# Attention's opening in another order, and the landmark sums of its second head group by other means

## The chip, the cores and the metric

The kernel runs on one core of a Trainium2 chip. The metric is the device time of one execution in microseconds, as the median of several runs. The engines are TensorE (PE in the profile, its weight loads PEld), VectorE (DVE), ScalarE (ACT), GpSimd (POOL) and SyncE (SP), which issues the DMAs.

## The reference

Three layers follow each other. The first is a Nyström attention over 4 batches, 8 heads, 576 tokens and 64 dimensions a head, with 32 landmarks that are means over 18 tokens; the other two are feed-forward layers over all 2304 tokens.

```
q_lm, k_lm = means of q and k over 18 tokens each
A  = softmax(scale * q    k_lm^T)
Bm = softmax(scale * q_lm k_lm^T)
C  = softmax(scale * q_lm k^T)
Z  = Bm^T / (norm1(Bm) * norminf(Bm) + 1e-6);  6 times: Z = 2Z - Z Bm Z
x  = A Z C v                       # 2304 tokens x 512
x  = mish(x w_in) w_out            # 512 -> 2048 -> 512
h  = x w2_in;  s = h * softmax(h);  out = (layernorm(s) * g_ln) w2_out
```

## The kernel before

The heads of a batch are worked on in two groups of four (g = 0 and 1). Batch 0 is done first, in small steps, so that the first feed-forward layer can begin; the other batches' attention is spread over that layer later. `A` of the attention is kept apart from the rest: the product of `Z C v` with the first weights is folded into a matrix `u` (`u_step`, L751), and the hidden layer is computed as `A^T` times `u` (`gemm1`, L760). All large products are split in a high and a low part, three products for one.

The weights arrive as 64-bit floats and are decoded on the chip, block by block (sixteen blocks of 1 MB for the first layer, in the order `order1`). A block goes through a scale step on ACT (`s`, L151), an exponent step on ACT (`e`, L159), one or two merges on DVE (`m`, `f`, L171 and L178) and, for the second weight matrix, a split on ACT and DVE (`m` ends with L252, `l` is L130).

The order of PE, ACT and DVE in the opening is written out by hand: `PSEQ` is a list of step names, and the instructions of each engine stand in the order in which the steps name them. No engine overtakes within its own queue. A trailing digit 0 or 1 after a name of the attention is the head group; for `s`, `e`, `f`, `m` and `l` it is the weight block, and for `G`, `M`, `S` and `Y` it is the pair of hidden tiles:

- `lq`, `lk`: landmark sums of q and k (`prep`). Group 0 sums on DVE (L386); group 1 has PE add up 18 products of the identity with every 18th column, 64 columns each (L383), and ACT copy the sum out (L384).
- `cs`, `as`, `bs`: the scores of C, A and Bm (L419, L512, L410). `cm`, `bm`: their maxima on DVE and exponentials on ACT (L461 to L468, L430 to L435). `bn`, `bu`, `bz`, `bb`, `ni`: norms of Bm, with column sums on PE (L447, L448), and the start of the iteration. `p1` to `p6` and `q1` to `q6`: its six steps, small products on PE (L328) and an addition on DVE (L130).
- `ct`, `cn`, `cv`: the transposed C, its row sums, and C v. `w`: the product with Z.
- `ta`, `tb` with a digit: transposition of the two halves of A's scores (L517). `sm`, `sn`, `sl`: softmax of the first half; `sx`, `sy`, `sz`: of the second. (`tb` without a digit loads ACT's table for Mish.)
- `u`, `u1`: folding of the weights. `G`, `M`, `S`, `Y`: hidden product, Mish (L789), split (L797 on ACT, L130 on DVE) and second product (L812) of a pair. `ld` is where SP issues the DMAs of six later weight blocks (into tiles that hold batch 0's q, k and v before).

Behind `PSEQ` the steps of the remaining pairs, decode steps and the other batches' attention are planned by counters. Those of them that the framework may move ahead are kept behind the step named `EDGE` (`Y1`). PSUM is taken in turn: four banks `y0` to `y3` for the attention's scores, a pair of banks `a`, and a tile `h` of two banks, of which there is one, so a hidden product waits until Mish has read the one before it.

Of the kernel before, what the change touches and what calls it, by code (L numbers as in the profile page):

```python
# [14 lines left out]
AF = mybir.ActivationFunctionType  # L15
ALU = mybir.AluOpType
AX = mybir.AxisListType
# [10 lines left out]
def nystrom_moe_kernel(  # L28
# [13 lines left out]
    V, A, PE, G, SP = nc.vector, nc.scalar, nc.tensor, nc.gpsimd, nc.sync  # L42
# [5 lines left out]
    L = 32  # L48
    R = S // L
# [27 lines left out]
    ident, swap = wheel[:, 0:P], wheel[:, D:]  # L77
# [154 lines left out]
    def w1_items():  # L232
        def item(side, m):
            if side == "i":
                s, a = divmod(m, 2)
                n = 2 * NQ
                return words((w_in, w_raw)[a](s)), w_in(s)[:, a * n:(a + 1) * n], lambda c: None, lambda c: None
            return parts(wr["o", m], wop, f"wo{m}", lambda x: wo.update({m: x}))

        return [lambda x=x: item(*x) for x in order1]  # L240
# [89 lines left out]
    def attn(b, g):  # L330
# [3 lines left out]
        T, lm, x = {}, {}, {}  # L334
# [9 lines left out]
        def ps(k=None):  # L344
            if first and k is None:
                bank_n[0] += 1
                return ps_y.tile([P, 512], F32, tag=f"y{bank_n[0] % 4}", name="pa")
            if first and k == "e" and g == 1:
                bank_n[1] += 1
                return ps_h.tile([P, 2, 512], F32, tag="h", name="pa")[:, bank_n[1] % 2]  # L350
            return ps_a.tile([P, 512], F32, tag="a", name="pa")
# [14 lines left out]
        def view_of(nm):  # L366
            T[nm] = raw[nm, b, g].rearrange("p (h s) -> p h s", h=2)

        def prep(nm):
            if nm not in T:  # L370
                view_of(nm)
            n = "qk".index(nm)
            if not lms or not first and not n:
                lms[:] = [att.tile([P, 2 * P + L], F32, tag="lm", name="lm")]
            t = x["lm"] = lms[0]
            if first:
                o = (2 * g + n) * 2 * L
                lm[nm] = t[:, o:o + 2 * L].rearrange("p (j h l) -> p j h l", j=1, h=2)
                src = T[nm].rearrange("p h (l r) -> p h l r", r=R)
                if g:  # L380
                    pt = ps("e")[:, 0:2 * L].rearrange("p (h l) -> p h l", h=2)
                    for r in range(R):
                        PE.matmul(pt, lhsT=ident, rhs=src[:, :, :, r], start=r == 0, stop=r == R - 1)  # L383
                    A.activation(out=lm[nm][:, 0], in_=pt, func=AF.Copy)  # L384
                else:
                    V.tensor_reduce(out=lm[nm][:, 0], in_=src, op=ALU.add, axis=AX.X)  # L386
            else:
                lm[nm] = t[:, n * P:(n + 1) * P].rearrange("p (j h l) -> p j h l", j=2, h=2)
                V.tensor_reduce(out=own(n), in_=T[nm].rearrange("p h (j l r) -> p h j l r", j=2, r=R), op=ALU.add, axis=AX.X)
            yield  # L390

        def own(n):

            d = x["lm"][:, n * P:(n + 1) * P + L].rearrange("p (j i) -> p j i", j=2)[:, :, 0:2 * L]
            return d.rearrange("p j (h l) -> p h j l", h=2)[:, :, :, 0:L // 2]
# [207 lines left out]
        def whole():  # L603

            yield from prep("q")
            for _ in prep("k"):
                cross()
                yield
# [31 lines left out]
        def opening():  # L640
# [55 lines left out]
            def soften(r0):  # L696
                sg[r0] = soft(r0, RH)
                next(sg[r0])
                next(sg[r0])

            r = {"lq": lambda: spin(prep("q")), "lk": lambda: spin(prep("k")), "bs": bs, "bm": bm, "bn": b_norm, "bb": bb, "bu": bu,
                 "bz": lambda: b_scale(px[1][:, 0:2 * L]), "ni": lambda: n_first(px[0]), "as": a_scores,
                 "ta": lambda: a_turn(0), "tb": lambda: a_turn(1), "sm": lambda: soften(0), "sn": lambda: next(sg[0]), "sl": lambda: spin(sg[0]),
# [21 lines left out]
    OWN = ()  # L725
    ONE = tuple(range(8))
    US = 1
    W2R = 0.6
    LAG = 3
    GB = 3  # L730
# [26 lines left out]
    def mm3(o, pairs):  # L757
# [4 lines left out]
    hb, gb, yb = {}, {}, {}  # L762
    ps_x = []
    PSEQ = """
        lq0 cs0 lk0 bs0 bm0 cm0 as0 lq1 tb0 bn0 ta0 s0 bb0 bu0 cs1 bz0 ct0 lk1 bs1 cn0 sm0 ni0 p10 cm1 bm1 q10 sn0 s1 p20 bn1 as1 bb1 e0 cn1 q20 e1
        s2 bu1 bz1 p30 q30 ni1 ct1 e2 tb1 p11 ta1 p40 q11 s3 p21 sx0 q40 e3 q21 sm1 p31 p50 cv0 q50 q31 m0 s4 p60 p41 q41 q60 p51 q51 cv1 e4 w0
        sn1 p61 q61 m1 w1 ld sl1 s5 sl0 u e5 G0 s6 m3 s7 sx1 tb M0 e6 m4 m2 m5 sy1 u1 l2 G1 M1 G2 S0 e7 S1 M2 l5 e8 m6 sz1
        Y0 sy0 G3 M3 sz0 s8 S2 l6 Y1 G4 S3 e9 M4 m7 Y2 G5 s9 l7 S4 M5 f8 Y3 m8 S5 f9 G6 Y4 M6 G7 Y5 m9 M7 S6"""
    GLB = 2
    HX = 1  # L770
    U = NCH * NF
# [60 lines left out]
    with ExitStack():  # L832
# [19 lines left out]
        w1, part = decode(w1_items(), lambda: att.tile([P, R * D], F32, tag="dc", name="dc", bufs=2)[:, 0:2 * DM], OWN, ONE, READY)  # L852
# [3 lines left out]
        def w1_tick():  # L856
            nonlocal done, ticks
            if done < NU:
                ticks += 1
                with behind():  # L860
                    done = next(w1, 10 ** 6)
# [132 lines left out]
        def may_step(u):  # L994
            b, s = steps[0]
            return all((b, g) in aw for g in range(NG)) and (b == 0 or last_use[b - 1, s] < u) and \
                (b > 0 or done > max(pos["i", i] for i in range(4 * s, 4 * s + 4)))

        for p in range(PAIRS, U // 2):
            u = 2 * p + 1  # L1000
            s_, i = units[u]
            c, i0, i1 = segs[s_]

            def tick():
                nonlocal w2n
                nonlocal k4
                if done < NU:
                    k4 += 1
                    want = NT * (p - PAIRS + k4 / 5) / DT
                    while ticks < want and done < NU:  # L1010
                        w1_tick()
                elif w2 and w2n < W2R * (u - w2u):
                    w2n += 1
# [6 lines left out]
            for x in '1sa.u..t2..u':  # L1020
# [10 lines left out]
                elif x == 'u':  # L1031
                    for _ in range(US):
                        if steps and may_step(u + 1):
# [212 lines left out]
```

## Time and profile before

| | us |
|---|---|
| median of 3 runs | 630.76 |
| lowest and highest | 628.88, 631.19 |
| the profiled execution | 628.73 |
| its span, first to last instruction | 627.0 |
| PE busy in the span | 601.1 |
| DVE busy | 374.2 |
| ACT busy | 330.2 |

The profiled execution is one run, and its span leaves out 1.7 us around the program. Busy times of PE are modelled from pipelined instructions, so a busy PE is not PE at its peak. Each written product of 32-bit floats stands as two records in the profile.

### The profile page before, as it was taken

What the parts mean: (1) busy time and instruction counts of PE and PEld (TensorE: products, weight loads), DVE (VectorE), ACT (ScalarE), POOL (GpSimd) and SP (SyncE); (2) the same over time, 40 slices, a digit from 0 to 9 for tenths busy, and PEclk for the clock granted to TensorE, in tenths of its full rate; (3) what the DMA queues carried; (4) which work ended last, traced back from release to release, by engine and by line L of the source; (5) the groups of instructions that cost most, each with busy time, mean ns of one, the idle gap of its engine ahead of it and who ended that gap; (6) DMA issues with size and microseconds to landing.
All of it is one profiled execution on the core that took longest, in us unless ns stands there. A gap on an engine that the chain in (4) does not pass through costs nothing.

```text
span 627.0 us, 11427 instructions
## 1 busy us (share of the span) xinstructions
PE 601.1 (96%) x4560; PEld 521.6 (83%) x4560; DVE 374.2 (60%) x868; ACT 330.2 (53%) x597; POOL 25.7 (4%) x21
## 2 busy tenths in 40 slices
PE   6888899999999999999999999999999999999997
PEld 4648878767999898999889999998888888888886
DVE  4787999755764224764456412555886667657560
ACT  2688975764563434553545533535665544536341
POOL 0000000000000000000132001230000000000000
PEclk9859999999999999999999999999999999999999
DMA  9997220521131100101253102411656444454442
GB/s 343 395 393 279 81 61 17 189 78 50 66 115 39 39 2 1 39 1 36 92 158 109 60 1 87 154 68 55 183 176 194 121 145 141 136 166 117 136 122 97
DMA packets 50453, 74.28 MB, mean 118 GB/s; under 512 B 5088, under 2 KB 38880, under 8 KB 50400
## 3 DMA queue, kind: packets, MB, share of 16 engines
q1 hardware_dynamic: 50400, 73.55, 35.9%
q8 instruction: 36, 0.59, 0.4%
q14 instruction: 17, 0.14, 0.1%
HBM read 54.07 MB, written 19.46 MB: 117 GB/s over the span
## 4 chain that ended last, share of the span: by engine, by line
PE 76%; ACT 9%; DVE 7%; DMA 4%; issue 2%; POOL 1%; POOLq 1%; SPq 0%; ACTq 0%; DVEq 0%
PE h L760 27%; PE y L812 24%; PE po L760 16%; PE pa L751 2%; DMA r<-in_moe_w_out_dram 2%; PE pa L383 1%; POOL r L149 1%; PE pa L500 1%; PE pa L419 1%; DMA r<-in_moe_w_in_dram 1%; ACT hl L252 1%; ACT ro L159 1%; PE pa L584 1%; ACT gh L797 1%; PE pa L328 1%
## 5 line engine op out<-in xcount | busy, mean ns | idle before, releaser
L812 PE MATMUL y<-gh,hl 128*128 128x288 f32 x1024 | 162.2, 298 | 2.6 <-DVE hl L130 1.4
L812 PEld LDWEIGHTS y<-gh,hl 128*128 128x128 f32 x1024 | 142.5, 188 | 13.5 <-issue 8.4
L760 PE MATMUL h<-AT,u 128*128 128x288 f32 x768 | 122.5, 303 | 6.7 <-ACT s L789 4.0
L760 PEld LDWEIGHTS h<-AT,u 128*128 128x128 f32 x768 | 107.3, 190 | 18.0 <-ACT s L789 6.9
L760 PE MATMUL h<-hl,yb 128*128 128x512 f32 x432 | 103.3, 395 | 0.1
L130 DVE SCALAR_TENSOR_TENSOR gl<-s,gh 128x288 fp32r<-128x288 f32 x128 | 53.3, 453 | 81.4 <-ACT gh L797 38.2
L760 PEld LDWEIGHTS h<-hl,yb 128*128 128x128 f32 x432 | 81.2, 188 | 19.3 <-ACT ye L829 0.5
L812 PE MATMUL y<-gl,hl 128*128 128x288 f32 x512 | 90.4, 297 | 0.0
L760 PE MATMUL po<-hl,lh 128*128 128x512 f32 x288 | 88.8, 389 | 0.0
L797 ACT ACTIVATE gh<-s 128x288 fp32r<-128x288 f32 x128 | 50.1, 440 | 48.5 <-PE y L812 48.2
L812 PEld LDWEIGHTS y<-gl,hl 128*128 128x128 f32 x512 | 74.8, 188 | 0.1
L789 ACT ACTIVATE s<-h 128x576 f32<-128x576 f32 x64 | 41.6, 650 | 59.6 <-PE h L760 49.9
L760 PEld LDWEIGHTS po<-hl,lh 128*128 128x128 f32 x288 | 54.1, 188 | 11.5
L1088 ACT ACTIVATE e<-h,st 128x1024 f32<-128x1024 f32 x18 | 20.1, 1117 | 71.9 <-DVE st L1087 71.9
L760 PE MATMUL po<-hl,ll 128*128 128x512 f32 x144 | 56.2, 390 | 0.0
L1086 DVE TENSOR_REDUCE st<-h 128x1 f32<-128x1024 f32 x18 | 22.0, 1223 | 33.7 <-PE h L760 33.7
L1139 DVE TENSOR_TENSOR ll<-lT,lh 128x1024 fp32r<-128x1024 f32 x18 | 22.1, 1225 | 19.1 <-ACT lh L1138 19.1
L130 DVE SCALAR_TENSOR_TENSOR u<-pa,u 128x512 fp32r<-128x512 f32 x32 | 20.7, 686 | 20.2 <-ACT u L754 20.2
L760 PEld LDWEIGHTS po<-hl,ll 128*128 128x128 f32 x144 | 27.0, 188 | 5.6
L178 DVE SCALAR_TENSOR_TENSOR r<-r 128x1024 uint32<-128x1024 uint32 x10 | 12.2, 1225 | 31.5 <-POOL r L149 31.5
L149 POOL TENSOR_SCALAR r<-r 128x1024 f32<-128x1024 f32 x8 | 23.3, 2909 | 139.9 <-DMA r<-in_moe_w_out_dram 58.1
L1096 ACT ACTIVATE s<-s,st 128x1024 f32<-128x1024 f32 x18 | 20.8, 1153 | 9.3 <-DVE st L1094 9.3
(180 smaller groups left out, 653.4 us busy)
## 6 DMA issues: line engine op xcount, KB each, us to landing
lnd<-sT SPq DMA_DIRECT2D x72, 128.0 KB, 2.3
lT<-lnd SPq DMA_DIRECT2D x18, 512.0 KB, 4.1
r<-in_moe_w_in_dram SPq DMA_DIRECT2D x8, 1024.0 KB, 8.2
ro<-in_moe_w_out_dram SPq DMA_DIRECT2D x8, 1024.0 KB, 16.0
yd<-ye SPq DMA_DIRECT2D x32, 144.0 KB, 1.8
y<-yd SPq DMA_DIRECT2D x18, 256.0 KB, 4.4
out_dram<-ob SPq DMA_DIRECT2D x18, 256.0 KB, 3.9
w<-in_moe_w_in_dram SPq DMA_DIRECT2D x4, 1024.0 KB, 10.8
```

Source lines behind the costliest of these rows:

```text
L130: return V.scalar_tensor_tensor(out=out, in0=in0, scalar=1.0, in1=in1, op0=ALU.mult, op1=op)
L149: G.tensor_scalar(out=x, in0=x, scalar1=2.0 ** -112, scalar2=None, op0=ALU.mult)
L178: V.scalar_tensor_tensor(out=t[:, :, 0], in0=t[:, :, 1], scalar=3, in1=t[:, :, 0], op0=ALU.logical_shift_left, op1=ALU.bitwise_or)
L751: PE.matmul(po[g][h * L:(h + 1) * L], lhsT=wb[b][r, g, h * L:(h + 1) * L], rhs=w[r, h], start=True, stop=True)
L760: PE.matmul(o, lhsT=a, rhs=b_, start=i == 0, stop=i == n - 1)
L789: A.activation(out=s, in_=h, func=AF.Mish)
L797: A.activation(out=gh[:, e], in_=s[:, e], func=AF.Copy)
L812: PE.matmul(yb[s_][d][:, 0:N], lhsT=w_out(s, i + e)[:, d * P:(d + 1) * P], rhs=r[:, e], start=i == i0 and e == k == 0, stop=i + 2 == i1 an ...
L1086: V.tensor_reduce(out=st[:, 0:1], in_=h, op=ALU.max, axis=AX.X)
L1088: A.activation(out=e, in_=h, func=AF.Exp, bias=st[:, 1:2], accum_out=st[:, 2:3])
L1096: A.activation(out=s, in_=s, func=AF.Identity, scale=-1.0, bias=st[:, 4:5])
L1139: V.tensor_tensor(out=llv, in0=src, in1=f(lhv), op=ALU.subtract)
```

## The change

Two things change. The sums of group 1: those of q are done by DVE, as for group 0. Those of k are done on PE by three products of the identity with 6 neighbouring columns of each landmark at a time (2 x 32 x 6 = 384 columns), which add up in PSUM and leave 6 partial sums for each landmark; DVE adds these, out of PSUM. And `PSEQ` has the same 141 names in another order.

```
-                if g:
-                    pt = ps("e")[:, 0:2 * L].rearrange("p (h l) -> p h l", h=2)
-                    for r in range(R):
-                        PE.matmul(pt, lhsT=ident, rhs=src[:, :, :, r], start=r == 0, stop=r == R - 1)
-                    A.activation(out=lm[nm][:, 0], in_=pt, func=AF.Copy)
+                if g and n:
+                    pt = ps("e")[:, 0:2 * L * GS].rearrange("p (h l s) -> p h l s", h=2, s=GS)
+                    n = R // GS
+                    for c in range(n):
+                        PE.matmul(pt, lhsT=ident, rhs=src[:, :, :, c * GS:(c + 1) * GS], start=c == 0, stop=c == n - 1)
+                    V.tensor_reduce(out=lm[nm][:, 0], in_=pt, op=ALU.add, axis=AX.X)
                 else:
                     V.tensor_reduce(out=lm[nm][:, 0], in_=src, op=ALU.add, axis=AX.X)
...
+    GS = 6
...
     PSEQ = """
-        lq0 cs0 lk0 bs0 bm0 cm0 as0 lq1 tb0 bn0 ta0 s0 bb0 bu0 cs1 bz0 ct0 lk1 bs1 cn0 sm0 ni0 p10 cm1 bm1 q10 sn0 s1 p20 bn1 as1 bb1 e0 cn1 q20 e1
-        s2 bu1 bz1 p30 q30 ni1 ct1 e2 tb1 p11 ta1 p40 q11 s3 p21 sx0 q40 e3 q21 sm1 p31 p50 cv0 q50 q31 m0 s4 p60 p41 q41 q60 p51 q51 cv1 e4 w0
-        sn1 p61 q61 m1 w1 ld sl1 s5 sl0 u e5 G0 s6 m3 s7 sx1 tb M0 e6 m4 m2 m5 sy1 u1 l2 G1 M1 G2 S0 e7 S1 M2 l5 e8 m6 sz1
-        Y0 sy0 G3 M3 sz0 s8 S2 l6 Y1 G4 S3 e9 M4 m7 Y2 G5 s9 l7 S4 M5 f8 Y3 m8 S5 f9 G6 Y4 M6 G7 Y5 m9 M7 S6"""
+        lq0 cs0 lk0 bs0 as0 lq1 bm0 cm0 bn0 ta0 cn0 s0 e0 bu0 cs1 bz0 sm0 e1 cm1 tb0 lk1 bb0 bs1 m0 ni0 bm1 ct1 p10 as1 sx0 bn1 q10 ta1 s1 bb1 bu1
+        ct0 s2 bz1 p20 q20 p30 ni1 p11 cn1 e2 q30 cv0 q11 sn0 p40 e3 q40 p21 s3 q21 e4 p31 sm1 p50 q31 s4 q50 p41 tb1 q41 p60 p51 q60 s5 q51 p61
+        m1 sn1 w0 cv1 q61 sl1 w1 ld e5 sx1 sl0 u s6 m3 s7 G0 tb m4 M0 m2 m5 sy0 l5 u1 sy1 l2 e6 G1 M1 S0 s8 S1 e7 G2 M2 e8
+        m6 sz0 Y0 sz1 f8 G3 e9 Y1 l6 M3 s9 S2 S3 G4 M4 Y2 m7 G5 S4 l7 M5 m8 Y3 G6 f9 S5 M6 Y4 G7 S6 M7 Y5 m9"""
```

## Rows read from the trace of the kernel before

**Rows 1.** The page, part 1: busy us (share of the span) xinstructions of each engine.

```profile
PE 601.1 (96%) x4560; PEld 521.6 (83%) x4560; DVE 374.2 (60%) x868; ACT 330.2 (53%) x597; POOL 25.7 (4%) x21
```

**Rows 2.** Table by stages: busy us (xinstructions) of each engine, granted clock, DMA.

```profile
core 0: us, PE busy (x) PEld busy (x) DVE busy (x) ACT busy (x) POOL busy (x), PEclk, DMA share, GB/s
11.00:22.10 11.10, 10.94 (x110) 9.82 (x109) 4.09 (x18) 2.12 (x6) 0.00 (x0) 1.00 1.03 377
22.10:50.30 28.20, 20.89 (x285) 12.42 (x285) 23.08 (x66) 26.10 (x44) 0.00 (x0) 0.70 1.03 400
50.30:60.00 9.70, 9.65 (x73) 9.65 (x74) 7.98 (x16) 6.76 (x12) 0.00 (x0) 1.00 0.79 313
60.00:105.00 45.00, 41.90 (x365) 36.97 (x364) 41.52 (x72) 34.63 (x59) 0.00 (x0) 1.00 0.18 55
105.00:300.00 195.00, 191.97 (x1894) 169.93 (x1891) 108.86 (x311) 100.02 (x216) 1.38 (x4) 1.00 0.16 53
```

**Rows 3.** Timeline of PE: start us, us, instruction, [idle before and its releaser].

```profile
50.35 1.87 PE L760 MATMUL h<-AT,u 128*128 128x288 f32 x12 [2.58 <-ACT s L789]
```

**Rows 4.** Timeline of ACT from 15 to 50 us, same columns.

```profile
15.04 0.22 ACT L384 ACTIVATE lm<-pa 128x64 f32<-128x64 f32 x1 [4.43 <-PE pa L383]
...
17.55 0.60 ACT L481 ACTIVATE scr_u<-pa 128x512 f32<-128x512 f32 x1 [1.27 <-PE pa L477]
18.05 0.26 ACT L482 ACTIVATE CT<-pa 64x128 f32<-64x128 f32 x1
21.98 0.22 ACT L384 ACTIVATE lm<-pa 128x64 f32<-128x64 f32 x1 [3.67 <-PE pa L383]
...
23.38 0.29 ACT L435 ACTIVATE scr_u<-pa,st 128x32 f32<-128x32 f32 x1
...
24.67 1.14 ACT L159 ACTIVATE w<-w 128x1024 uint32<-128x1024 uint8 x1
...
26.71 1.12 ACT L151 ACTIVATE ro<-ro 128x1024 f32<-128x1024 f32 x1
...
49.65 0.65 ACT L789 ACTIVATE s<-h 128x576 f32<-128x576 f32 x1
```

**Rows 5.** Chain of waits in order of time: start us, us, what.

```profile
5.84 2.14 PE pa L419 x16
...
8.09 1.92 PE pa L512 x16
10.01 5.00 PE pa L383 x36
...
15.27 0.34 PE pa L447 x2
...
15.83 1.10 PE pa L419 x16
...
17.63 4.33 PE pa L383 x36
```

**Rows 6.** DMA issues at 2.6 and at 16.3 us: KB, us to landing.

```profile
w<-in_moe_w_in_dram SPq DMA_DIRECT2D x1, 1024.0 KB, 8.9
...
ro<-in_moe_w_out_dram SPq DMA_DIRECT2D x1, 1024.0 KB, 17.9
```

**Rows 7.** Timeline of DVE from 4 to 19 us, columns as for PE.

```profile
4.24 2.84 DVE L386 TENSOR_REDUCE lm<-scr_w 128x64 f32<-128x1152 f32 x2 [2.15 <-DMA scr_w<-in_q_dram]
...
11.32 0.24 DVE L444 TENSOR_SCALAR rs<-diag,st 128x32 f32<-128x32 f32 x1
...
18.26 0.81 DVE L461 TENSOR_REDUCE st<-pa 128x1 f32<-128x288 f32 x2
```

**Rows 8.** Table by stages around the low clock, columns as before.

```profile
22.00:28.00 6.00, 4.25 (x89) 2.58 (x89) 4.96 (x25) 6.00 (x13) 0.00 (x0) 1.00 1.02 408
29.00:45.00 16.00, 13.51 (x170) 8.02 (x176) 13.43 (x32) 13.91 (x21) 0.00 (x0) 0.50 1.04 392
46.00:62.00 16.00, 13.41 (x99) 13.08 (x100) 11.82 (x25) 13.06 (x23) 0.00 (x0) 1.00 0.75 299
```

## The prediction

> **What bounds the kernel now.** I read the page first. TensorE is busy for 96% of the span [rows 1], so the time is TensorE's own work plus the holes in it, and the question is where the holes are. The table by stages answers it: from 105 to 300 us TensorE is busy for 191.97 of 195 us, from 60 to 105 for 41.90 of 45, and from 50.3 to 60 for 9.65 of 9.70; but between 22.1 and 50.3 only for 20.89 of 28.20 [rows 2]. From the third hidden product on (PE at 50.35) TensorE has so little slack that what it gains there should stay gained to the end. So I look for what sets the start of that product, and follow it backwards.
>
> It waited 2.58 us for ACT's second Mish [rows 3], which began at 49.65 [rows 4]. In the stage before it ACT is the full engine: 26.10 of 28.20 us busy from 22.1 to 50.3, while from 11 to 22.1 it had worked 2.12 of 11.10 us [rows 2]. ACT's string therefore starts at about 22 and is then worked off almost without a break. What held it up stands in its timeline: 4.43 us of waiting that end at 15.04 and 3.67 us that end at 21.98, both for L383, the landmark sums of group 1 on TensorE [rows 4]. The chain of waits says the same from TensorE's side: the 36 records of q's sums are 5.00 us of it and those of k 4.33 us [rows 5]. Behind them stand decode steps (scale, exponent) whose data are there already: the first weight block lands 8.9 us after its issue at 2.6, so at 11.5 [rows 6], and ACT takes its second block's scale only after 23.38 and the two exponent steps at 24.67 [rows 4].
>
> So the kernel's opening is a serial stage (sums, then scores, then softmax, then Newton) that keeps ACT empty until 22, then an ACT-bound stage to 50, then a TensorE-bound one to the end.
>
> **The change part by part.** *The sums of q, group 1, go to VectorE.* The 36 records, 5.00 us of TensorE, go away [rows 5], as does a small ACT copy. VectorE pays one reduction of 1152 elements; two of these took 2.84 us [rows 7], so 1.4 us each. It comes at about 7.3, when q of group 1 has landed, and VectorE has time there (4.09 of 11.10 us busy just after, [rows 2]). It does delay group 0's softmax: the string of small VectorE steps that ended at 11.56 (L444, [rows 7]) waited for scores that TensorE finished at 8.09 [rows 5], and the reduction ends at 8.7, so 0.6 us later, of which the transposition that the new order puts behind this string gives back about as much. I put its end at 11.7; the bounds are 11.1 and 13.0 (nothing, or all of the 1.4 added).
>
> *The sums of k, group 1, become three wide products.* The written number falls from 18 to 3, the columns stay 1152. The trace has no such product; bounds: above, the 4.33 us that the narrow ones take [rows 5]. Below, the cost per column where weights are loaded seldom: L419's scores stream 2 x 288 columns of the same type one half after the other in 1.10 us at 15.83 and in 2.14 us at 5.84 [rows 5], so 1.9 and 3.7 ns a column, which makes 2.2 and 4.3 us for 1152. The same instructions at two prices are the two levels of TensorE's clock, 2.4 and 1.2 GHz. (The granted clock is recorded as 0.50 only from 29 to 45 [rows 8]; the first L419 shows by its price that it was low at the start too.) VectorE then reduces 384 elements out of PSUM; 288 took 0.41 us (L461, two in 0.81, [rows 7]), and each further one some 1.1 ns by the difference to 1152, so 0.5 us, between 0.4 and 1.4.
>
> *When k's landmarks are ready.* Before: 22.20 (ACT's copy at 21.98 + 0.22, [rows 4]). In the new order TensorE does the column sums (bu0) at 11.7, 0.6 us (15.27 to 15.83, [rows 5]), then group 1's scores (cs1), then the wide products. High clock throughout: 11.7 + 0.6 + 1.1 + 2.2 + 0.5 = 16.1. Low throughout: 11.7 + 0.6 + 2.1 + 4.3 + 0.5 = 19.2. Which level? In the kernel before, scores and sums ran one behind another from 5.84 to 15.01 [rows 5]; now TensorE pauses from 10.0 to 11.7, so I don't count on a high clock at once, and take low for cs1 and halfway (3.2) for the wide products: 18.1, which is 4.1 us earlier than before. The Trainium skill ("TensorE: Matmul & The Clock Gate", section "What's actually happening") speaks against this change here: the low clock is the default, and only activity lifts it, while the change takes out the densest early work. By that rule alone the sum would use 19.2 and lose another 1.1 us; by the high price of the later L419 it would use 16.1 and win 2.0. The profile of before agrees with the rule as far as its clock fell after a stretch of small products (22 to 28, TensorE 4.25 of 6 us busy) [rows 8].
>
> *From there to ACT's second Mish.* Before, the exponent of group 1's middle matrix (23.38) came 1.2 us after the landmarks [rows 4]. The new order puts a merge of decoded words (m0, 1.1 us) and Newton's start (ni0, 0.4) on VectorE between them, so 1.9 us: 18.1 + 1.9 = 20.0, which is 3.4 earlier than 23.38. Then ACT works off the same list up to its second Mish, but for what was moved across this point: the two exponent steps e0 and e1 (24.67 to 26.71, 2.0 us, [rows 4]) are done earlier, in the hole after 11.5, and the evacuation of group 0's transposed scores (ct0, 17.55 to 18.31, 0.8 us, [rows 4]) comes later. Net 1.2 less. The other moved steps (e5, sx1, s0, cm1, sm0) stay on their side of it or within ACT's free time, and cost nothing as long as ACT has a backlog; without one each would cost its own 0.4 to 1.1 us. So the second Mish comes 3.4 + 1.2 = 4.6 us earlier, at 45.0. The two bounds, from 16.1 and 19.2, are 6.6 and 3.5. The waits that ACT kept inside the stretch (2.10 us, [rows 2]) I leave as they are.
>
> *What could refuse the gain.* Weights: eight of the sixteen blocks are needed before this Mish. The last of these is issued at about 16.3 and lands 17.9 us later, at 34.2 [rows 6]; behind it ACT needs only some 7 us to the second Mish, so that is no bound. The DMA engines stay full until 57 whatever the order (share 1.03, [rows 2]); moving the point where SyncE issues the later blocks (ld) a few us earlier only lengthens their queue, and what is queued behind it (the next batch's v) is needed long after. VectorE: 1.9 us more in all, in its free time before 22; if that cover were gone, it would be 1.9 us of a stage where VectorE is full (41.52 of 45, [rows 2]). The reorder after 45 (s8 earlier, Y1 later, S2 and S3 together) moves steps between engines that all have a backlog; I price it at nothing, bounds 1 us either way, the length of one decode step.
>
> **Sum.** TensorE's third hidden product starts 4.6 us earlier, and the rest follows. The profiled execution took 628.73 us (span 627.0 and 1.7 around it), so 624.1; against the median of 630.76, which lies 2.0 above the profiled one, **626.2**. Its own range is 624.2 to 627.8 (gains of 6.6 and 3.0, the lower with the 0.5 that the reorder may take).
>
> **The rivals.** 0.5%, about 3.15 us, is what a measurement of this kernel can tell from no change.
>
> *The gain is eaten on the way.* VectorE is 92% and ACT 77% busy from 60 to 105, TensorE 93% [rows 2]. If VectorE, not TensorE, sets the pace there, then the 1.9 us that it got extra count, and any step that the new order puts at a wrong place among the later planned steps costs up to its length. Half the gain would go: about 628.5 to 631. For it: the high share of VectorE. Against: VectorE's own backlog is also worked off earlier, because it starts earlier. Chance 0.2 (with the case in which the wide products run no faster than 4.3 us and the softmax string ends at 13.0: then the landmarks come at 20.5, the gain is 2.2 to 2.9, the time 628 to 628.6).
>
> *The clock falls later, into the TensorE-bound stage: slower.* Before, the low clock lay on 28 to 45, where TensorE had slack; from 46 on it was high [rows 8]. With the dense sums gone, the low stretch may begin at another time. If it is as long as that of before (17 us) and begins at 42 or later, all of it lies behind the third hidden product, where each us of work takes two: 8.5 us lost, 4.6 won, and about 1 us returned because the first products of the hidden layer run at the high clock: 630.76 - 4.6 - 1 + 8.5 = 633.7. It decides from more than 9 us of low clock after 45 on: less, and the kernel is still faster. The rule of the Trainium skill cited above ("TensorE: Matmul & The Clock Gate") would lead here, if the small Newton products count as little activity. Against: the first hidden products and the folding of the weights (u, G0, u1) are dense and precede the third; before, the clock had come back right after them. Chance 0.1. A short overlap, some 6 us, costs 3 and ends at 629.2: chance 0.1, no change.
>
> *The change doesn't do what it says.* ACT's hole might simply move: VectorE now stands between group 1's sums and everything else, and if ACT waits for VectorE after 18 as it waited for TensorE, no time is won: 630 to 632. Chance 0.05.
>
> **How the numbers follow.** Forecast 0.55. Eaten 0.2, of which half falls within 0.5% and a quarter each to the sides. Clock 0.1 slower and 0.1 no change; moved hole 0.05, mostly no change. Faster by over 0.5%: 0.55 and 0.05, so 0.6. Within: 0.1 + 0.1 + 0.05, and a little of the forecast's lower end that falls under 3.15, 0.27. Slower: 0.13. The range reaches from the forecast's upper gain and a little (a high clock from 11 on and a better reorder, 623.0) to the no-change cases, 631.5.
>
> **What would show it.** In the profile after: no L383 records for q, six for k in 2.2 to 4.3 us before 19.2; ACT's wait for L383 gone and its first long wait over by 12; e0 and e1 before 15; the second Mish near 45 and TensorE's third hidden product right behind; from there TensorE as dense as before. Wrong if the second Mish is early and the span is not (then something behind 60 took it back), if the granted clock reads 0.50 beyond 48, or if ACT's share between 20 and 45 falls clearly under 90% with VectorE named as what it waits for.

## The result and the profile after

The changed kernel takes **622.81 us** (median of 6 runs, 622.63 to 623.11), the kernel before 630.11 beside it (6 runs, 628.88 to 632.12): a ratio of 0.9884, 95% interval 0.9866 to 0.9902. The forecast was 626.2 with a range of 623.0 to 631.5: the direction was right, the time lies 0.2 us below the range, and the gain is 7.3 us. The profiled execution took 622.86 us, its span is 621.1. So 5.87 us lie between the two profiled executions (628.73 and 622.86), and the medians stand 1.4 us further apart than these.

The page's part 1 of the profile after, to compare with [rows 1]: busy us, share of the span, instructions.

```profile
PE 596.4 (96%) x4494; PEld 514.3 (83%) x4494; DVE 376.6 (61%) x870; ACT 330.4 (53%) x595; POOL 25.6 (4%) x21
```

TensorE has 4.7 us less work and the span is 5.9 shorter. It is tempting to take the one for the other; the experiments will show a kernel with less work of this kind and no gain.

The table by stages of the profile after, columns as in [rows 2]. The second and third row divide the stage 22.1 to 50.3 of before at the new second Mish.

```profile
core 0: us, PE busy (x) PEld busy (x) DVE busy (x) ACT busy (x) POOL busy (x), PEclk, DMA share, GB/s
11.00:22.10 11.10, 9.80 (x79) 4.86 (x79) 7.73 (x28) 6.63 (x17) 0.00 (x0) 1.00 1.03 382
22.10:45.00 22.90, 17.87 (x257) 11.04 (x253) 20.93 (x59) 21.59 (x32) 0.00 (x0) 0.70 1.03 396
45.00:50.30 5.30, 3.96 (x25) 3.48 (x26) 5.20 (x12) 5.30 (x10) 0.00 (x0) 1.00 1.03 410
...
60.00:105.00 45.00, 42.27 (x369) 36.62 (x367) 42.31 (x71) 32.93 (x56) 0.00 (x0) 1.00 0.20 62
105.00:300.00 195.00, 193.78 (x1907) 172.71 (x1906) 104.97 (x307) 98.19 (x216) 1.72 (x5) 1.00 0.17 53
```

The first row is the change: from 11 to 22.1 us ACT works 6.63 us where it worked 2.12, and VectorE 7.73 where it worked 4.09. ACT is 4.5 us of work ahead, and VectorE about 3, as 0.56 of its 3.64 us are the new reduction out of PSUM. ACT is as full as before up to its second Mish (21.59 of 22.90 us).

Timeline of VectorE after, from 8 to 19 us (answers to [rows 7]):

```profile
8.21 1.35 DVE L387 TENSOR_REDUCE lm<-scr_u 128x64 f32<-128x1152 f32 x1 [1.24 <-DMA scr_u<-in_q_dram]
...
11.61 0.24 DVE L445 TENSOR_SCALAR rs<-diag,st 128x32 f32<-128x32 f32 x1
...
18.66 0.56 DVE L385 TENSOR_REDUCE lm<-pa 128x64 f32<-128x384 f32 x1 [2.87 <-PE pa L384]
```

Timeline of TensorE after (answers to [rows 3] and [rows 5]):

```profile
12.47 2.15 PE L420 MATMUL pa<-scr_u,lm 64*32 64x288 f32 x16
14.55 4.07 PE L384 MATMUL pa<-scr_u,wheel 128*128 128x384 f32 x6
...
46.05 1.87 PE L762 MATMUL h<-AT,u 128*128 128x288 f32 x12 [2.10 <-ACT s L791]
```

Timeline of ACT after (answers to [rows 4]; its L436 is L435 of before, its L791 is L789):

```profile
12.21 1.14 ACT L151 ACTIVATE w<-w 128x1024 f32<-128x1024 f32 x1 [0.27 <-DMA w<-in_moe_w_in_dram]
13.23 1.13 ACT L159 ACTIVATE w<-w 128x1024 uint32<-128x1024 uint8 x1
14.33 0.44 ACT L532 ACTIVATE Aw<-Aw 128x288 f32<-128x288 f32 x1
14.83 1.14 ACT L159 ACTIVATE r<-r 128x1024 uint32<-128x1024 uint8 x1
...
21.05 0.29 ACT L436 ACTIVATE scr_u<-pa,st 128x32 f32<-128x32 f32 x1 [4.13 <-DVE st L432]
...
45.37 0.63 ACT L791 ACTIVATE s<-h 128x576 f32<-128x576 f32 x1
```

The three wide products stand as six records of 4.07 us, so 3.5 ns a column, the dearer of the two prices. ACT starts its decode at 12.21, and the wait for L383 at 15.04 is gone. One wait of 4.13 us remains, before the exponent of group 1's middle matrix, but three decode steps lie ahead of it. The second Mish begins at 45.37 and was at 49.65.

What of that reaches the end is read by the start of each hidden product in the two traces. The third is 4.30 us earlier (50.35 to 46.05), the seventh 3.54, the tenth 5.95, the seventeenth 5.80 (144.08 to 138.28), and from there on the distance stays between 5.6 and 5.9. It is not one constant shift: it sinks and grows between 50 and 90 us.

From the third to the seventeenth hidden product TensorE does the same work in both kernels. The table by stages of that stretch, first before and then after:

```profile
50.35:144.08 93.73, 88.12 (x878) 74.31 (x878) 75.90 (x153) 67.58 (x121) 0.40 (x1) 1.00 0.31 103
46.05:138.28 92.23, 88.52 (x879) 74.48 (x879) 74.97 (x151) 67.31 (x121) 0.21 (x1) 1.00 0.37 125
```

It is 1.5 us shorter after: TensorE's idle time in it falls by 1.9 us, from 5.61 to 3.71, and its work takes 0.4 longer.

### The profile page after: what moved, and what is told of

It reads as the page before. It is cut to its first block, busy times and chain, and to the rows that moved or that the text cites. A ratio compares the mean times of both kernels' runs of the same rounds, so it can differ in the third digit from the quotient of the medians.

```text
span 621.1 us, 11293 instructions
## 1 busy us (share of the span) xinstructions
PE 596.4 (96%) x4494; PEld 514.3 (83%) x4494; DVE 376.6 (61%) x870; ACT 330.4 (53%) x595; POOL 25.6 (4%) x21
## 4 chain that ended last, share of the span: by engine, by line
PE 85%; DVE 6%; ACT 4%; DMA 3%; POOL 1%; issue 1%; SPq 0%; ACTq 0%; POOLq 0%; DVEq 0%
PE h L762 31%; PE y L814 30%; PE po L762 16%; PE pa L753 2%; DMA scr_u<-in_q_dram 1%; POOL r L149 1%; PE pa L420 1%; DMA r<-in_moe_w_in_dram 1%; PE pa L585 1%; PE pa L501 1%; DMA r<-in_moe_w_out_dram 1%; PE pa L384 1%; PE pa L328 1%; DVE r L178 1%; DVE cc L171 1%
## 5 line engine op out<-in xcount | busy, mean ns | idle before, releaser
L814 PE MATMUL y<-gl,hl 128*128 128x288 f32 x512 | 92.3, 299 | 0.0
L791 ACT ACTIVATE s<-h 128x576 f32<-128x576 f32 x64 | 41.7, 651 | 59.8 <-PE h L762 47.3
L1141 DVE TENSOR_TENSOR ll<-lT,lh 128x1024 fp32r<-128x1024 f32 x18 | 22.1, 1225 | 20.3 <-ACT lh L1140 20.3
## 6 DMA issues: line engine op xcount, KB each, us to landing
ro<-in_moe_w_out_dram SPq DMA_DIRECT2D x8, 1024.0 KB, 16.3
```

What stands on the lines that cost most here:

```text
L791: A.activation(out=s, in_=h, func=AF.Mish)
L814: PE.matmul(yb[s_][d][:, 0:N], lhsT=w_out(s, i + e)[:, d * P:(d + 1) * P], rhs=r[:, e], start=i == i0 and e == k == 0, stop=i + 2 == i1 an ...
L1141: V.tensor_tensor(out=llv, in0=src, in1=f(lhv), op=ALU.subtract)
```

## The experiments

Each was timed on one chip with the kernel before, and its trace read against those of before and after.

**Each part alone, and the order in two halves.** sums_only is the changed kernel with the old `PSEQ`; order_only the kernel before with the new one. head_new has the new sums, the new order up to `M1`, and the remaining names in the order of before; tail_new the old sums, the old order up to `M1`, and the rest in the new one:

```
sums_only   after.py,  PSEQ = that of before
order_only  before.py, PSEQ = that of after
head_new    after.py,  PSEQ = new up to M1, then "G2 S0 e7 S1 M2 e8 m6 sz1 Y0 G3 M3 sz0 s8 S2 ..." (old)
tail_new    before.py, PSEQ = old up to M1, then "sy0 l5 S0 s8 S1 e7 G2 M2 e8 m6 sz0 Y0 sz1 ..." (new)
```

> Old written order, new sums alone. Opening theory (the gain is made before TensorE's third hidden product and only carried from there): k's landmarks come at about 19 instead of 22.2, the exponent steps e0 and e1 stay where they were, so the third hidden product comes some 3 us earlier and the time is 627. Store theory (a further 1.5 us comes at 65 to 80 us, because the four stores of yp no longer stand between loads in SyncE's queue, as they also don't in this kernel): 625.5.

> New written order, old sums. Opening theory: the 5.0 and 4.3 us of narrow products are back on TensorE, the third hidden product moves by less than 1 us, time 629.5. Store theory: SyncE's queue has the stores together here too, so 1.5 us less, 628. If the order is what wins, rather than the sums: 626 or less.

> New sums and new order up to the second Mish, the old order behind it; SyncE's queue has the four yp stores each between loads here. Opening theory: third hidden product 4.3 us earlier as in the changed kernel, and the time 625.8 if everything behind is only carried, 623 to 624 if ACT and DVE, which are ahead too, give TensorE fewer waits later. Store theory: the 1.5 us of the stretch from 65 to 80 us are missing, 625.8 or more.

> Old sums and old order up to the second Mish, the new order behind it; SyncE's queue has the four yp stores together, as in the changed kernel. Opening theory: nothing is won, 629.5 to 631. Store theory: 1.5 us won, 628.6, and the hidden products 7 to 9 of the trace gain what those of the changed kernel gained there. Tail theory (the order of the steps behind the second Mish itself wins the rest): 628.6 too, but with the gain at another place than the stores.

Measured: sums_only 629.24 (ratio 0.998, 0.996 to 1.000), order_only 632.51 (1.004, 1.002 to 1.006), head_new **622.71** (0.988, 0.986 to 0.991), tail_new 631.23 (1.002, 1.000 to 1.004).

So neither part gains alone, and both together in the opening gain everything; the reorder behind `M1` is worth nothing within the error. The 627 expected of sums_only and the 629.5 of order_only were both missed; the store theory, which wanted 625.8 or more of head_new and 628.6 of tail_new, has fallen with these two, and so has the tail theory. Why the sums alone do nothing is seen where the landmarks are waited for. Timeline of VectorE in sums_only:

```profile
19.71 0.56 DVE L385 TENSOR_REDUCE lm<-pa 128x64 f32<-128x384 f32 x1 [5.22 <-PE pa L384]
```

Timeline of ACT in sums_only:

```profile
21.59 0.44 ACT L532 ACTIVATE Aw<-Aw 128x288 f32<-128x288 f32 x1 [4.10 <-DVE Aw L130]
...
23.86 0.29 ACT L436 ACTIVATE scr_u<-pa,st 128x32 f32<-128x32 f32 x1
```

In the old order VectorE's next instruction behind its group 0 softmax is the reduction of k's partial sums. It stands 5.22 us at the head of VectorE's queue, and all that ACT could do meanwhile is queued behind it there. The landmarks come 1.9 us earlier than before and the exponent comes at 23.86 instead of 23.38 [rows 4]: the wait has moved from ACT to VectorE, as the rival of the moved hole had it. This kernel's TensorE is busy for 601.0 us, as before, though it has the same instructions as the changed kernel with 596.4: its clock was low from 21.8 to 45.6 and twice more. Table by stages of sums_only:

```profile
21.80:45.60 23.80, 19.75 (x253) 11.68 (x253) 19.66 (x63) 20.12 (x34) 0.00 (x0) 0.50 1.03 397
52.50:55.80 3.30, 3.30 (x16) 3.30 (x15) 3.30 (x7) 3.00 (x5) 0.00 (x0) 0.50 1.02 408
113.90:117.30 3.40, 3.40 (x27) 2.20 (x26) 3.37 (x8) 0.24 (x1) 0.00 (x0) 0.50 0.37 87
```

In order_only the narrow sums stand in the way. Timeline of ACT in order_only:

```profile
15.20 0.22 ACT L384 ACTIVATE lm<-pa 128x64 f32<-128x64 f32 x1 [12.99 <-PE pa L383]
...
24.52 0.22 ACT L384 ACTIVATE lm<-pa 128x64 f32<-128x64 f32 x1 [2.79 <-PE pa L383]
```

ACT's copy of q's sums (12.99 us of waiting) is ahead of the first scale step in its queue, so the step that the new order calls early starts at 16.54, and the second copy is 2.5 us later than before. (Of its ten executions two, the profiled one among them, took 628.4 and 629.0, at a mean clock of 0.986, seven 632.2 to 633.9, at 0.975 to 0.978, and one 638.4: its loss against before goes with a lower clock, but none of the seven was profiled.)

**The clock at the start.** k_on_dve does k's sums by VectorE too, so that TensorE has no landmark sums at all:

```
-                if g and n:
+                if False:
```

> The changed kernel with the sums of k, too, by one reduction on VectorE (1.35 us in place of the wide products, 4.07 us of TensorE at the low clock, and their reduction of 0.56). Landmark theory (the wide products are now on the path to ACT's string): k's landmarks at 17.1 instead of 19.2, third hidden product up to 2 us earlier, time 621 to 622. VectorE theory: 0.8 us more on VectorE, but early, where it has holes; end 621.5 to 623. Clock rule: with these products gone too the clock stays low for longer, and the time is 623 to 626.

Measured 623.98 (0.991, 0.988 to 0.994): 1.2 us slower than the change by the medians, with overlapping intervals, and not faster. The same 32 small products of C v, by the timelines of TensorE, first in k_on_dve and then in the profile after:

```profile
24.64 1.08 PE L501 MATMUL pa<-v,scr_u 128*32 128x64 f32 x32
```

```profile
25.21 0.65 PE L501 MATMUL pa<-v,scr_u 128*32 128x64 f32 x32
```

Without the wide products TensorE was at the dear price there, with them at the cheap one (0.65 us in six more traces of kernels with the changed opening, 1.01 in after_hold2). The landmarks were ready at 16.56 instead of 19.22, but ACT then waited 2.2 us for the transposed scores of C from TensorE, 0.5 in the profile after, and the second Mish came at 45.29, as in the profile after (45.37). In this trace the work taken off TensorE was paid back in its clock.

**The pace behind the third hidden product.** Four kernels add or remove work there. after_dve puts nine small reductions on VectorE behind `Y0`, and after_pe ten products of the identity on TensorE (their results are unused). after_less leaves out part of the computation: batch 1's landmark sums run over 2 of the 18 tokens, 4.3 us less for VectorE (0.28 instead of 1.35 us each, between 56 and 97 us in the profile after); before_less is the same edit of the kernel before.

```
+            for _ in range(9):
+                V.tensor_reduce(out=junk, in_=ident.rearrange("p (h l) -> p h l", h=HG), op=ALU.add, axis=AX.X)
...
+            for _ in range(10):
+                PE.matmul(t[:, 0:P], lhsT=ident, rhs=ident, start=True, stop=True)
...
-                V.tensor_reduce(out=own(n), in_=T[nm].rearrange("p h (j l r) -> p h j l r", j=2, r=R), op=ALU.add, axis=AX.X)
+                V.tensor_reduce(out=own(n), in_=T[nm].rearrange("p h (j l r) -> p h j l r", j=2, r=R)[:, :, :, :, 0:R if b > 1 else 2], op=ALU.add, axis=AX.X)
```

> The changed kernel with nine more small reductions on VectorE (0.28 us each, about 2.2 us together, their result unused) behind the first second-layer product Y0. VectorE theory (from 50 to about 145 us VectorE's backlog sets the pace, so the gain at the end is what VectorE gained, not what TensorE gained): the time rises by 1.5 to 2.2 us, to 624.5 or 625. TensorE theory (what TensorE gains at the third hidden product is carried to the end): less than 0.7, at most 623.5.

> The changed kernel with ten more products of the identity with itself on TensorE (about 2.1 us together, result unused) behind Y0. TensorE theory: the time rises by 2 us, to 625. VectorE theory: TensorE has slack there, it rises by less than 0.7, to 623.5 at most.

> The changed kernel in which the four landmark sums of batch 1 (VectorE, 1.34 us each, between 53 and 96 us) add up 2 of the 18 tokens; this part of the computation is left out, about 4.7 us of VectorE. VectorE theory (VectorE sets the pace there): the time falls by 2 us or more, to 620 or 621, until another engine holds it. TensorE theory: it falls by less than 0.5.

> The kernel before with the same part left out (2 of 18 tokens in the four landmark sums of batch 1, between 64 and 103 us). VectorE theory: it too gets faster, by 2 us or more, to 628 or less. If VectorE was not the pace of the kernel before, less than 0.5.

Measured: after_dve 626.47 (0.993), 3.7 us slower than the change for 2.85 us of added work; after_pe 623.95 (0.992), 1.1 slower for 2.39; after_less 622.55, no gain over the change; before_less 628.23 (0.997, 0.995 to 1.000), some 1.8 faster than the kernel before beside it. So added work on VectorE costs much of its length or all of it (in its trace the fifth hidden product waits 2.47 us for Mish and then takes 3.21 us, in a stretch of low clock, so some 1.5 of the 3.7 us may be the clock's), and on TensorE about half by the medians and more by the trace: against another execution of the change with the same opening (after_again below, third hidden product at 44.64 and here at 44.50) 1.9 of the 2.39 us are left at 302 us. But less work for VectorE is not given back in the changed kernel. Timeline of TensorE in after_less:

```profile
44.10 2.68 PE L762 MATMUL h<-AT,u 128*128 128x288 f32 x12 [3.25 <-ACT s L791]
...
64.25 0.52 PE L814 MATMUL y<-gh,hl 128*128 128x288 f32 x2 [2.18 <-DVE hl L130]
```

Behind both waits stands a stretch of half clock (44.8 to 48.2 and 65.3 to 68.7), where the profile after has none, and VectorE, two reductions lighter by then, waits 1.05 us for ACT at 59.83. So after_less doesn't decide: VectorE is not the pace all along, since it waits for ACT, but what it gained may also have gone to the clock.

**Less for VectorE, by GpSimd.** low_on_pool moves the low parts of the second weights' blocks to GpSimd:

```
+                if pool is wop:
+                    G.tensor_tensor(out=x[:, :, 1], in0=c, in1=f(x[:, :, 0]), op=ALU.subtract)
```

> The changed kernel with the low part of each block of the second weights (eight subtractions of 128 x 1024, 1.14 us each on VectorE) done by GpSimd, which is idle until 120 us; all of the computation is there. VectorE theory: up to 9 us of VectorE go, GpSimd takes about 3 us for each but has the time, and the time falls by 1 to 4 us, to 619 to 622. TensorE theory: no change, or a loss of 1 to 2 us because the second products Y0 to Y3 wait for the slower low parts.

Measured 631.85 (1.003), 9 us slower than the change: a step takes 2.6 us on GpSimd (8 in 20.9 us), and TensorE waits for it. Timeline of TensorE in low_on_pool:

```profile
68.70 0.53 PE L817 MATMUL y<-gh,hl 128*128 128x288 f32 x2 [2.33 <-POOL hl L262]
```

**TensorE's wait filled, and its start held back.** before_fill gives the kernel before eight products of the identity between `G1` and `G2`, in the 2.58 us wait of [rows 3], which leaves 0.79 us of it. after_hold2 and after_hold4 put 17 and 26 of them at the same place of the changed kernel, more than its 2.10 us wait takes, so that only the third hidden product comes later while ACT and VectorE go on as they were.

```
+            for _ in range(17):
+                PE.matmul(t[:, 0:P], lhsT=ident, rhs=ident, start=True, stop=True)
```

> The kernel before with eight products of the identity with itself between the first hidden products, in the 2.6 us in which TensorE waits for the second Mish; nothing else is changed. Clock theory of the spread (the executions of the kernel before fall in two groups, 628.4 to 629 at a mean clock of 0.983 to 0.986 and 631 to 632 at 0.974 to 0.977, and the slow ones lose the clock for 3.4 us behind this wait, as the traces of the old head with new sums and of the new order with old sums show at 51 to 56 us): the slow group goes, median 628.6. Rival (the spread has another cause, in the DMAs for one): both groups stay, median 630; if the products end later than the Mish, 630.5.

> The changed kernel with 17 products of the identity with itself on TensorE between the second and the third hidden product, 4.1 us by 0.244 us each, of which 2.1 us fill the wait that is there (their result is unused). The third hidden product should start some 2 us later, at about 48. Theory of the prediction (what TensorE gains at the third hidden product stays gained): the end is 2.0 us later, about 624.8. Theory that TensorE still has slack behind it, because VectorE's and ScalarE's strings started earlier too and these are not delayed: at most half is lost, 622.8 to 623.8.

> The same with 26 products, 6.3 us: the third hidden product should start some 4.2 us later, at about 50.2, where the kernel before has it, while all that VectorE and ScalarE gained up to there is kept. Theory of the prediction: the end is 4.2 us later, about 627.0, so only what the clock gives (up to 2 us against the median of before) is left of the gain. Rival (the gain comes by VectorE's and ScalarE's earlier start as much as by TensorE's): half is lost, about 624.9; with no loss by TensorE at all, 622.8.

Measured: before_fill 628.5 (0.999, 0.998 to 1.001), after_hold2 623.92 (0.990, 0.986 to 0.993), after_hold4 623.82 (0.990, 0.986 to 0.994; five executions, of which two took 627.0 and 627.6). Timeline of TensorE in after_hold2:

```profile
47.10 1.85 PE L762 MATMUL h<-AT,u 128*128 128x288 f32 x12
...
64.63 0.53 PE L815 MATMUL y<-gh,hl 128*128 128x288 f32 x2 [1.12 <-DVE hl L130]
...
79.44 0.40 PE L762 MATMUL h<-AT,u 128*128 128x288 f32 x1 [0.69 <-ACT u L756]
```

And in the profile after:

```profile
64.95 0.54 PE L814 MATMUL y<-gh,hl 128*128 128x288 f32 x2 [1.58 <-DVE hl L130]
...
79.40 0.40 PE L762 MATMUL h<-AT,u 128*128 128x288 f32 x1 [0.69 <-ACT u L756]
```

The third hidden product comes 1.05 us later than in the profile after (47.10 against 46.05), while ACT's second Mish is 0.30 earlier, so it is held back by 1.3 us. At 64.6 that is gone: TensorE waits there for the low part of a weight block from VectorE, 1.12 us instead of 1.58, and goes on 0.32 earlier than in the other execution. At 79.4 both wait 0.69 us for ACT's `u` and start within 0.04 of each other. At 302 us the shift is 0.07. In after_hold4 the opening ran better (second Mish 1.35 earlier) and the product is 1.53 later, held back by 2.9; at 302 us 0.7 later is left. (This is the execution of 627.6: its end is 4.5 us later, most of that by a wait of 2.16 us for ACT that ends at 390.90 and a stretch of half clock behind it, where the profile after waits 0.50 us and keeps its clock.) So of a delay of TensorE alone a part is made good by its next waits for ACT and VectorE: 0.1 to 0.4 us are left of 1.3, and 0.7 to 2.1 of 2.9, by whether the opening's own lead would have been kept not at all or in full. The execution of the change in the next paragraph, with its second Mish within 0.1 us of that of after_hold4, speaks for the upper end: against it the third product is 2.94 later, and 1.9 are left at 302 us. The medians are 1.1 and 1.0 us above the change's. The prediction's theory asks for all of the delay, 1.3 and 2.9 us as it came out; the median of after_hold2 alone would allow that, that of after_hold4 and the two traces don't. So some 0.5 to 1 us of a delay of TensorE alone is made good behind the third product, by after_pe and after_hold4.

**The changed kernel once more**, to see how its own executions differ:

> The changed kernel once more, beside the next three on the same chip: 622.8. Its executions should not fall in two groups as those of the kernel before do.

Measured 622.44 (0.989, 0.986 to 0.992): three executions at 621.9 to 622.8, and a fourth at 624.87, with a mean clock of 0.978 instead of 0.986 to 0.988. So the expectation was missed by one execution in four, and the distance between executions is rarer in the changed kernel, not gone. In its profiled execution (span 620.3) the third hidden product is at 44.64, 1.4 us earlier than in the first, at 302 us 1.2 of these are left, and the end is 0.8 earlier; in head_new's it is at 43.95 and the end is 0.7 earlier (span 620.4). Here, too, only a part of what the third product gains stays.

## Why the prediction was off

**What held: the opening, step by step.** Group 0's string of small VectorE steps ended at 11.85 (predicted 11.7). Its new reduction took 1.35 (1.4), at 8.21 and not at 7.3, because q lands later. Group 1's scores took 2.15 (2.1). The reduction out of PSUM took 0.56 (0.5). Group 1's exponent came 1.83 us behind the landmarks (1.9), ACT did e0 and e1 before 16 and not before 15, since the first scale step went ahead of them. The second Mish began at 45.37 (45.0) and the third hidden product 4.30 us earlier (4.6).

**What varies there: the wide products.** I took 3.2 us, halfway between the two prices; in the profiled execution they took 4.07, so the landmarks were ready at 18.66 + 0.56 = 19.22 and not at 18.1: the sum's own upper bound of 19.2, that with the low clock throughout. The 1.1 us lost at the landmarks were mostly regained up to the second Mish, as ACT's waits between 22.1 and 45.0 came to 1.31 us and not to the 2.10 that I had left as they were. But the profiled execution is one of those with the latest openings. Nine of the kernels traced have the changed opening up to the second hidden product. Timeline of TensorE in head_new:

```profile
12.93 2.27 PE L384 MATMUL pa<-scr_u,wheel 128*128 128x384 f32 x6
...
43.95 1.88 PE L762 MATMUL h<-AT,u 128*128 128x288 f32 x12 [2.19 <-ACT s L792]
```

Timeline of TensorE in after_again:

```profile
14.02 3.06 PE L384 MATMUL pa<-scr_u,wheel 128*128 128x384 f32 x6
...
44.64 1.87 PE L762 MATMUL h<-AT,u 128*128 128x288 f32 x12 [2.66 <-ACT s L791]
```

The wide products took 2.27 us in three of the nine traces, 3.0 to 3.1 in three and 4.0 to 4.2 in three, so both prices and the middle that I took. With them the landmarks were ready between 15.5 and 19.2, the second Mish began between 43.2 and 45.4, and the third hidden product, where nothing holds it back, started 4.3 to 6.4 us earlier than before: the bounds that the sum had were 3.5 and 6.6. The Trainium skill ("TensorE: Matmul & The Clock Gate", section "What's actually happening") says that the low clock is the default and activity lifts it. The trace of k_on_dve agrees, with the dear price still at 24.64. What sets the nine apart no run shows: the pause of TensorE ahead of the column sums was 1.52 us in the profile after (4.07), 1.65 in after_again (3.06) and 0.42 in after_hold2 (4.21).

**The step that failed: "TensorE's third hidden product starts 4.6 us earlier, and the rest follows", and with it the sum against the median.** It has two halves.

First, the median of before stands 2.0 us above its profiled execution, and I carried that over to the changed kernel as a constant. It is none: the changed kernel's median (622.81) is its profiled time (622.86). This is 2.0 of the 3.4 us between 626.2 and 622.8; some 0.65 of the 2.0 come of the three executions taken, as the median of before was 630.76 in three and 630.11 in six. Where before's 2.0 come from shows in its executions. Of 25 beside sums_only the five fastest, 628.4 to 628.7, had a mean granted clock of 0.983 to 0.986, and the seven with 0.974 to 0.977 took 631.0 to 631.8. (The clock isn't all of it: two at 0.986 took 630.5 and 630.7, one at 0.984 634.6, and none of those above 630 was profiled.) A single stretch of low clock makes such a difference, as the profiled execution of after_hold2 shows (626.46, against 623.4 to 624.0 of its other three). Table by stages of it:

```profile
318.00:321.48 3.48, 1.47 (x12) 1.24 (x10) 2.98 (x5) 1.70 (x3) 0.00 (x0) 1.00 0.77 268
321.48:324.90 3.42, 3.42 (x15) 3.42 (x16) 2.55 (x5) 1.81 (x5) 2.75 (x1) 0.51 0.31 78
324.90:330.00 5.10, 5.10 (x49) 4.62 (x50) 3.19 (x4) 3.19 (x6) 0.21 (x1) 0.99 0.00 0
```

Timeline of TensorE there:

```profile
321.43 3.16 PE L762 MATMUL h<-AT,u 128*128 128x288 f32 x12 [2.01 <-ACT s L792]
```

And in the profile after:

```profile
320.79 1.85 PE L762 MATMUL h<-AT,u 128*128 128x288 f32 x12 [1.43 <-ACT s L791]
```

A wait of 2.01 us, then 3.4 us at half the clock, and a hidden product that takes 3.16 us instead of 1.85. The shift against the profile after goes from 0.07 at 313 us to 2.2 at 328 by this, 0.6 of it by the longer wait. That before meets such stretches more often than the changed kernel is read from the clocks alone (0.974 to 0.986 against 0.984 to 0.989 in nine of the ten runs of the changed one, 0.978 in the tenth); why it does stays open. before_fill, which takes 1.8 us of the wait of [rows 3] away, still had three of ten runs above 630.

Second, the shift of 4.3 us at the third hidden product became 5.9 at the end, where "the rest follows" had it equal, and 5.9 against the 4.6 forecast is the other 1.3 us (624.1 was forecast against the profile, 622.86 came). In the profiled execution of after_again 5.7 us at the third product became 6.6 at the end, in that of head_new 6.4 became 6.5. So the lead is carried in all three and the end lies 5.9 to 6.6 us before that of the profile before, whether the third product is 4.3 or 6.4 us earlier; 4.6 was too small for this, and the third product alone doesn't give the end. The premise was that TensorE has so little slack behind this product; but of the 93.73 us to the seventeenth it was idle for 5.61, and in the profile after 1.9 of these are gone. The kernels that hold this product back show, too, that its start does not alone set what follows: TensorE's next waits hang on the strings of ACT and VectorE, which the change moved ahead too. Before had four such waits between 60 and 105 us (at 63.10, 68.50, 75.90 and 84.77, 2.9 us in all), the profile after three (at 64.95, 79.40 and 103.06, 2.5 us). So the direction and the opening were forecast by the right mechanism, and the carrier was too narrow: the third product's wait for Mish told of ACT's lead, but was not the only gate to the end. Between 105 and 144 us before has waits of 0.95 and 0.61 us that the profile after doesn't have (TensorE busy 193.78 against 191.97 of 195 us from 105 to 300, [rows 2]). Which engine's lead takes each of these waits away no run divides: added VectorE work costs, removed VectorE work does not always pay.

**The rivals.** "Eaten on the way" was right that VectorE counts behind 60 (after_dve: 3.7 us for 2.85), and wrong in its outcome, because VectorE's string started earlier, as was said against it. "The clock falls later" did not come: 0.50 from 28.6 to 42.2 and 1.00 from there on. Table by stages of the profile after, answering to [rows 8]:

```profile
18.30:28.50 10.20, 7.22 (x191) 4.56 (x190) 9.27 (x38) 6.99 (x13) 0.00 (x0) 1.00 1.03 406
28.50:42.20 13.70, 11.81 (x113) 6.39 (x106) 12.27 (x26) 12.94 (x20) 0.00 (x0) 0.50 1.04 390
42.20:60.00 17.80, 15.41 (x110) 14.70 (x111) 15.97 (x30) 16.61 (x27) 0.00 (x0) 1.00 1.00 391
```

In smaller form, as short stretches, it came behind 45 us in several of the traces (57.2 in after_dve, 44.8 and 65.3 in after_less). The "moved hole" is what sums_only does, and the new order is what prevents it in the changed kernel: transposition, exponentials, norms and three decode steps, which VectorE and ACT can do meanwhile, stand ahead of the reduction or of ACT's wait for it. The reorder behind `M1`, priced at nothing with 1 us either way, was worth nothing (head_new).

## What to carry to other kernels

A sum made against one profiled execution gives the time of such an execution; before adding the distance to the median, ask whether what makes that distance (here stretches of low clock behind TensorE's waits) will be there in the changed kernel. The wait that ends last is a sign of who leads, not proof that its end carries to the finish: where two engines feed a third over tens of us, a delay of the third alone can be made good in part at its next waits (here 0.5 to 1 us of it). One profiled execution can lie at the edge of what its kernel does: read a second before calling a term mis-sized. When a producer is made faster, look at what stands in the consumer's queue behind the instruction that waits for it: here the faster sums alone gave 0.7 us, within the interval nothing, and the new order alone lost 2.6, and both together gained 7.3.

## What the runs showed of the hardware

Short stretches of half clock (some 3.4 us each, one of 6.8) lay mostly at a wait of TensorE. The wait's end and the start of the stretch: 44.10 (3.25 us of waiting) and 44.8 in after_less, 45.99 (3.07) and 46.6 in k_on_dve, 51.64 (2.58) and 52.5 in sums_only, 55.06 (1.84) and 55.9 in tail_new, 57.12 (2.47) and 57.2 in after_dve, 68.70 (2.33) and 69.2 in low_on_pool, 321.43 (2.01) and 321.6 in after_hold2, 390.90 (2.16) and 391.2 in after_hold4. Timeline of TensorE in tail_new:

```profile
55.06 0.77 PE L813 MATMUL y<-gl,hl 128*128 128x288 f32 x2 [1.84 <-DVE gl L130]
```

Table by stages of tail_new:

```profile
50.00:55.90 5.90, 3.23 (x20) 2.82 (x21) 5.80 (x12) 4.58 (x9) 0.00 (x0) 1.00 1.02 408
55.90:59.30 3.40, 3.40 (x16) 3.40 (x15) 2.30 (x5) 2.70 (x4) 0.00 (x0) 0.50 1.01 362
```

Behind 38 us the sixteen traces have 22 waits of TensorE of 1.8 us or more, and 13 of them have such a stretch at or within 3 us behind their end. The other nine don't (2.58 us at 50.35 in the profile before, 2.10 at 46.05 in the profile after, 2.66 at 44.64 in after_again: the clock stays at 1.00), and two stretches, from 113.9 in sums_only and from 104.7 in head_new, lay behind waits of 0.35 and 0.95 us. A wait of 2 us that looks harmless in one profile can so cost another 1.3 us or more in the next execution of the same kernel.

The rows of the clock begin late: the table names 1.00 from 11 to 18.3 us after, while TensorE's own prices there (2.15 us for scores that took 1.10 at 15.83 in [rows 5]) are those of the low level. In the opening the price of a known instruction is the better clock. In k_on_dve the rows begin only at 39.7, so that its mean clock of 0.997 leaves the low opening out: mean clocks can be compared only where the rows begin alike.
